# Layer 1 of a fused retention kernel takes its first two token blocks in turns, one weight chunk at a time

## The chip, the cores and the metric

The kernel runs on one core of a Trainium2 chip. The time is that of one launch on the device, in microseconds (us). TensorE does the matrix products; VectorE (DVE in the profile), ScalarE (ACT) and GpSimd (POOL) do the elementwise work; SyncE (SP) issues the transfers between DRAM and the core's memory.

## What is computed

A retention block and two layers, on 4 x 576 = 2304 tokens:

```python
scores = scale * np.matmul(q, k.transpose(0, 1, 3, 2))        # 4 batches, 8 heads, 576 x 576, head size 64
ret = scores * Dmat                                            # gamma_h ** (i - j) for i >= j, else 0
x = np.matmul(ret, v)                                          # -> 2304 tokens x 512
h = x @ w_in1;  x = (h * np.tanh(softplus(h))) @ w_out1        # layer 1: 512 -> 2048 -> 512, Mish
h = x @ w_in2;  out = (h / (1 + np.exp(-1.702 * h))) @ w_out2  # layer 2: 512 -> 2048 -> 512
```

The weights arrive as 64-bit floats and are turned into 32-bit ones on the core. For precision each operand of a layer's product is kept as a high part that TensorE takes and a low part, the rest; a product is made of three (high x high, high x low, low x high: PARTS).

## The kernel before

**Retention** (attention(), L678) walks 20 units: 4 batches of five chunks of tokens, four of 128 and one of 64. A unit's q, k, v are one transfer of 1 MB (0.5 MB for the short one) into one of four buffers (load, L682; load(u + 3) is issued in iteration u). TensorE makes scores (L738), the state's update (L761) and the outputs (L786, L797); VectorE masks the scores (L742) and writes x (finish, L811); POOL scales v (decay_v, L727). In iterations 17 and 18 the first two up-products of layer 1 follow.

**Layer 1** goes over SLOTS: one slot is one block of tokens (BLOCKS, 512 or 256 wide) with one chunk m of the 2048 hidden values (16 chunks of 128). In step i TensorE does up(i), 12 products into a PSUM bank, and down(i - 3), 12 products onto four accumulators (LAG = 3); elementwise(i) puts Mish on ScalarE, splits the result g into high (ScalarE) and low (VectorE, or POOL for i < POOL_SLOTS = 9). The order before, with m in brackets: block 0 [0-7], block 1 [0-15], block 0 [8-15], block 2 (256 wide) [0-15], block 3 [0-7], block 4 [0-15], block 3 [8-15]. A slot that begins another block needs its x split into high and low first (split_x, L336), into buffers that the last up of the block before must have left; the accumulators of a block that ends are moved to X by VectorE (evacuate, L378).

**Chunks.** A chunk's weights (1 MB of 64-bit words) are fetched in two halves into the buffer of the next chunk (fetch, L166) and turned by convert (L224), each half in stages that are spread over the following steps: clamp (L189, VectorE), rest and rebase (ScalarE for chunks 0 to 5; rebase on VectorE, L194, from chunk 6 on), sign (L134, L201, VectorE), join (L205, POOL), the high part (ScalarE), the low part by subtraction (L247, VectorE for chunks 0 to 5, POOL from 6 on). EARLY = 6 chunks are fetched during retention, one every three units from unit 2 on; the others start at the slots LATE. plan() gives each job its step and position() runs it there: "fetch", "pool", "act early", "vector", "act late" are fixed places in every step. The program order of each engine is written out by hand in this way (manual_schedule), and each engine works its own in order.

**Layer 2's weights** are prepared during slots PREP_FIRST = 23 to PREP_LAST = 67 (prepare, L255: 32 jobs, four buffers "cr") and written to DRAM as a stream that layer 2 (second_layer, L530) reads back.

## Time and profile before

| | us |
|---|---|
| runs | 852.04, 853.03, 854.59; median 853.03 |
| the profiled execution | 857.23, its span 855.4 |
| TensorE busy (PE) | 830.4 (97%) |
| VectorE busy (DVE) | 585.8 (68%) |
| ScalarE busy (ACT) | 389.5 (46%) |
| GpSimd busy (POOL) | 153.7 (18%) |

The profile is one execution; its span goes from the first to the last event on the core. PE is a product on TensorE, PEld the load of its weights; busy shares are means over the three stages. L352 is line 352 of the kernel, and one line can be a helper's: L125 is every ScalarE operation. A wait in brackets names what ended it.

### The profile page before, as it was taken

What the parts mean: (1) busy time and instruction counts of PE and PEld (TensorE: products, weight loads), DVE (VectorE), ACT (ScalarE), POOL (GpSimd) and SP (SyncE); (2) the same over time, 40 slices, a digit from 0 to 9 for tenths busy, and PEclk for the clock granted to TensorE, in tenths of its full rate; (3) what the DMA queues carried; (4) which work ended last, traced back from release to release, by engine and by line L of the source; (5) the groups of instructions that cost most, each with busy time, mean ns of one, the idle gap of its engine ahead of it and who ended that gap; (6) DMA issues with size and microseconds to landing.
All of it is one profiled execution on the core that took longest, in us unless ns stands there. A gap on an engine that the chain in (4) does not pass through costs nothing.

```text
span 855.4 us, 13241 instructions
## 1 busy us (share of the span) xinstructions
PE 830.4 (97%) x4966; PEld 749.3 (88%) x4966; DVE 585.8 (68%) x1047; ACT 389.5 (46%) x722; POOL 153.7 (18%) x154
## 2 busy tenths in 40 slices
PE   8898999999999989999999999999999999999998
PEld 5776878887887988888888899999999999999997
DVE  3697797973477876778863445588755699555776
ACT  3453544443353645455543333366333565233553
POOL 2353484642121112323310000000000000000000
PEclk9999999999999999999999999999999999999999
DMA  7899530001146775659832247778878678877774
GB/s 294 323 357 371 220 127 1 1 1 49 50 149 200 249 240 156 202 181 283 250 117 93 99 148 258 258 229 273 273 267 272 235 248 281 302 243 257 239 258 167
DMA packets 97839, 175.80 MB, mean 206 GB/s; under 512 B 5616, under 2 KB 68720, under 8 KB 92272
## 3 DMA queue, kind: packets, MB, share of 16 engines
q1 hardware_dynamic: 97776, 174.97, 60.7%
q8 instruction: 39, 0.64, 0.3%
q14 instruction: 24, 0.20, 0.1%
HBM read 140.87 MB, written 34.08 MB: 205 GB/s over the span
## 4 chain that ended last, share of the span: by engine, by line
PE 82%; DMA 6%; DVE 5%; ACT 3%; issue 2%; POOL 1%; SPq 0%; ACTq 0%; POOLq 0%; DVEq 0%
PE acc L370 20%; PE p L583 19%; PE h L352 19%; PE p L639 19%; DMA unit<-qkv_dram 5%; PE sc L738 1%; PE o L786 1%; PE o L797 1%; ACT g L125 1%; ACT cr L125 1%; PE ds L761 1%; POOL cy L205 1%; DVE cr L134 1%; DMA cr<-w_dram 1%; DVE g L429 1%
## 5 line engine op out<-in xcount | busy, mean ns | idle before, releaser
L352 PE MATMUL h<-x,w 128*128 128x512 f32 (+1 forms) x960 | 215.3, 373 | 6.4 <-ACT x L125 2.4
L370 PE MATMUL acc<-g,w 128*128 128x512 f32 (+1 forms) x960 | 212.4, 371 | 0.3 <-DVE X L388 0.3
L352 PEld LDWEIGHTS h<-x,w 128*128 128x128 f32 x960 | 169.6, 191 | 40.1 <-DVE x L340 3.1
L370 PEld LDWEIGHTS acc<-g,w 128*128 128x128 f32 x960 | 170.1, 190 | 31.6 <-issue 0.5
L639 PE MATMUL p<-g,ring 128*128 128x384 f32 x1008 | 178.8, 336 | 1.9 <-ACT g L125 0.9
L639 PEld LDWEIGHTS p<-g,ring 128*128 128x128 f32 x1008 | 174.3, 188 | 6.0 <-DVE g L429 2.4
L583 PE MATMUL p<-xop,ring 128*128 128x384 f32 x1008 | 175.2, 334 | 0.0
L583 PEld LDWEIGHTS p<-xop,ring 128*128 128x128 f32 x1008 | 174.8, 188 | 0.1
L125 ACT ACTIVATE g<-cs 128x384 fp32r<-128x384 f32 x168 | 86.9, 523 | 62.5 <-PE p L639 60.8
L429 DVE TENSOR_TENSOR g<-cs,g 128x384 fp32r<-128x384 f32 x168 | 91.8, 556 | 31.8 <-ACT g L125 31.0
L398 DVE TENSOR_TENSOR g<-c,g 128x512 fp32r<-128x512 f32 (+1 forms) x71 | 48.5, 683 | 83.3 <-ACT g L125 83.3
L125 ACT ACTIVATE g<-c 128x512 fp32r<-128x512 f32 (+1 forms) x80 | 47.2, 589 | 127.5 <-PE acc L370 127.1
L125 ACT ACTIVATE cs<-cs 128x384 f32<-128x384 f32 x72 | 37.8, 526 | 118.7 <-DVE cs L429 118.7
L205 POOL TENSOR_TENSOR cy<-cr 128x256 int32<-128x256 int32 x64 | 51.2, 820 | 159.6 <-DVE cr L201 75.7
L125 ACT ACTIVATE c<-h 128x512 f32<-128x512 f32 (+1 forms) x80 | 44.0, 550 | 56.0 <-PE h L352 55.2
L429 DVE TENSOR_TENSOR cs<-cs 128x384 f32<-128x384 f32 x96 | 53.1, 553 | 0.8
L125 ACT ACTIVATE cr<-cr 128x512 int32<-128x512 uint32 (+1 forms) x68 | 40.8, 650 | 0.5 <-DVE cr L189 0.5
L292 DVE TENSOR_TENSOR cy<-cy,cr 128x896 fp32r<-128x896 f32 x32 | 37.9, 1191 | 4.4 <-ACT cr L125 3.5
L429 DVE TENSOR_TENSOR u<-p,s 128x384 f32<-128x384 f32 x30 | 16.7, 556 | 35.3 <-PE p L583 35.3
L205 POOL TENSOR_TENSOR raw<-raw 128x512 int32<-128x512 int32 x30 | 34.5, 1150 | 34.8 <-DVE raw L201 34.8
L285 DVE TENSOR_TENSOR cy<-cy 128x128 f32<-128x128 f32 x96 | 25.4, 292 | 16.8 <-POOL cy L205 15.7
L125 ACT ACTIVATE cr<-cy 128x896 fp32r<-128x896 f32 x32 | 29.9, 942 | 12.9 <-DVE cy L286 12.9
(62 smaller groups left out, 680.1 us busy)
## 6 DMA issues: line engine op xcount, KB each, us to landing
ring<-stream SPq DMA_DIRECT2D x112, 512.0 KB, 4.5
ring<-stream SPq DMA_DIRECT2D x28, 1024.0 KB, 4.8
cr<-w_dram SPq DMA_DIRECT2D x32, 512.0 KB, 4.2
unit<-qkv_dram SPq DMA_DIRECT2D x15, 1024.0 KB, 6.8
raw<-w_dram SPq DMA_DIRECT2D x30, 512.0 KB, 8.9
stream<-cr SPq DMA_DIRECT2D x32, 448.0 KB, 2.9
stream<-cy SPq DMA_DIRECT2D x32, 448.0 KB, 3.3
unit<-qkv_dram SPq DMA_DIRECT2D x6, 512.0 KB, 5.9
```

The source lines that it names most:

```text
L125: nc.scalar.activation(out=o, in_=i, func=f, scale=scale, bias=bias)
L134: nc.vector.scalar_tensor_tensor(out=o, in0=i0, scalar=s, in1=i1, op0=op0, op1=op1)
L205: nc.gpsimd.tensor_tensor(out=o, in0=upper, in1=bits, op=ALU.add)
L285: nc.vector.tensor_tensor(out=v[:, o], in0=v[:, a], in1=v[:, b], op=op)
L292: nc.vector.tensor_tensor(out=y, in0=v, in1=hi.bitcast(F32), op=ALU.subtract)
L352: nc.tensor.matmul(h[:, :n], lhsT=W[m][:, a, k * P : (k + 1) * P], rhs=xs[k][:, b, :n], start=((k, a, b) == order[0]), stop=((k, a, b) == ...
L370: nc.tensor.matmul(acc[e][:, :n], lhsT=W[m][:, a, DM + e * P : DM + (e + 1) * P], rhs=g[:, b, :n], start=(begins(i) and a == 0 and b == 0) ...
L398: lambda: eng.tensor_tensor(out=g[:, 1, :n], in0=c[:, :n], in1=g[:, 0, :n].bitcast(F32), op=ALU.subtract),
L429: eng.tensor_tensor(out=o, in0=a, in1=b, op=op)
L583: nc.tensor.matmul(banks[p], lhsT=w[:, a, k * P : (k + 1) * P], rhs=x[:, b, k], start=(p not in SAME and k == 0 and a == 0 and b == 0), st ...
L639: nc.tensor.matmul(banks[e, p], lhsT=w[:, a, e * P : (e + 1) * P], rhs=g[:, b], start=(p != 2 and r == 0 and a == 0 and b == 0), stop=(r = ...
L738: nc.tensor.matmul(sc[j][:n, p, :n], lhsT=kt[sl, p, :], rhs=qt[sl, p, :], start=True, stop=True)
```

## The change

- SLOTS: the blocks are now 512, 256, 512, 512, 512 wide. Blocks 0 and 1 (SIDE, 256 wide) take turns: chunk 0 for block 0, chunk 0 for block 1, chunk 1 for block 0, and so on. Then block 2 takes all chunks, block 3 half of them, block 4 all, block 3 the other half. A slot has a third field, the stretch it belongs to, by which begins() and ends() go.
- SIDE's x stands in two buffers of its own ("side0", "side1"), split in retention at units 13 to 16 (X_UNITS); its accumulators share two banks (b4, b5), so that "up" has two banks, b6 and b7, until four slots after the pair.
- The x of block 2 is split in elementwise(30), one slot before the pair ends.
- EARLY: 4 chunks in retention instead of 6, one every four units, converted five units later; the other 12 are planned 1.95 slots apart from slot 1. Chunk 15 comes in halves instead of quarters.
- The unit buffers: five instead of four, load(u + 4) in iteration u.
- rebase is always on ScalarE, the weight subtractions and the g subtractions always on VectorE.
- Layer 2's weights are prepared over slots 28 to 68. The "cr" buffers are two; the other two jobs of four use side0 and side1 once the pair is done. Later the same two hold a tile each of layer 2 (g2, t3); "u4" has two buffers.

```diff
--- before.py
+++ after.py
@@ -26,35 +26,26 @@
 CH = [(c, min(P, S - c)) for c in range(0, S, P)]
 NCH = len(CH)
 UNITS = [(b, c) for b in range(B) for c in range(NCH)]
-BLOCKS = [(0, 512), (512, 512), (1024, 256), (1280, 512), (1792, 512)]
-PAIRS = [(0, 1), (3, 4)]
-OTHER = {t: u for p in PAIRS for t, u in (p, p[::-1])}
+BLOCKS = [(0, 512), (512, 256), (768, 512), (1280, 512), (1792, 512)]
+SIDE, WIDTH = 1, 256
+OTHER = {3: 4, 4: 3}
 HALF = NM // 2
-def slots():
-    order = []
-    for t in range(len(BLOCKS)):
-        if any(t == p[0] for p in PAIRS):
-            order += [(t, range(HALF)), (t + 1, range(NM)), (t, range(HALF, NM))]
-        elif t not in OTHER:
-            order.append((t, range(NM)))
-    return [(t, m) for t, ms in order for m in ms]
-SLOTS = slots()
+SLOTS = [(t, m, t) for m in range(NM) for t in (0, SIDE)] + [(2, m, 2) for m in range(NM)]
+SLOTS += [(3, m, 3) for m in range(HALF)] + [(4, m, 4) for m in range(NM)] + [(3, m, 5) for m in range(HALF, NM)]
+BOTH = 2 * NM
 def begins(i):
-    return i < len(SLOTS) and (i == 0 or SLOTS[i][0] != SLOTS[i - 1][0])
+    return i < len(SLOTS) and all(SLOTS[j][2] != SLOTS[i][2] for j in range(i))
 def ends(i):
-    return 0 <= i < len(SLOTS) and (i + 1 == len(SLOTS) or begins(i + 1))
+    return 0 <= i < len(SLOTS) and all(s[2] != SLOTS[i][2] for s in SLOTS[i + 1 :])
 def sources(o, n):
@@ -68,9 +59,11 @@
 LAG = 3
 KEPT = 10
-EARLY = 6
-EARLY_FIRST, EARLY_EVERY = 2, 3
-LATE = (1, 3, 5, 6.5, 8, 10, 12, 14, 15.5, 17)
+X_UNITS = (6, 8, 10, 12, 13, 14, 15, 16)
+EARLY = 4
+EARLY_EVERY, EARLY_AFTER = 4, 5
+LATE = [1 + 1.95 * i for i in range(NM - EARLY)]
+UNITS_AHEAD = 4
@@ -89,9 +82,8 @@
 UP_STEPS = NR * NP
 STEPS = 2 * UP_STEPS
 AHEAD = 3
-PREP_FIRST, PREP_LAST = 23, 67
+PREP_FIRST, PREP_LAST = 28, 68
 X_FIRST = 75
-POOL_SLOTS = 9
 WARM = 3
@@ -208,23 +200,18 @@
         lower, bits = words(raw)[:2]
         act(bits, lower, scale=2.0**-29)
-    def parts(m, i, q):
+    def parts(m, i):
         if m not in W:
             W[m] = place(m).tile([P, 2, 2 * DM], F32R, tag=f"w{m}", name=f"w{m}")
-        n = q * DM // 2
-        w = W[m][:, :, i * n : (i + 1) * n].rearrange("p r (q n) -> p r q n", q=q)
+        w = W[m][:, :, i * DM : (i + 1) * DM].rearrange("p r (q n) -> p r q n", q=2)
         return w[:, 0], w[:, 1]
-    def quarter(m, j):
-        raw = temp[0].tile([P, 1, DM // 2], I64, tag="cr", name="cr", bufs=4)
-        nc.sync.dma_start(out=raw[:, 0], in_=w1[m][:, j * DM // 2 : (j + 1) * DM // 2])
-        return raw
-    def convert(m, i, q, engine):
-        if q == 1:
-            raw = quarter(m, i)
+    def convert(m, i):
+        if m == NM - 1:
+            raw = temp[0].tile([P, 2, DM // 2], I64, tag="cr", name="cr", bufs=2)
+            nc.sync.dma_start(out=raw, in_=w1[m][:, i * DM : (i + 1) * DM].rearrange("p (q n) -> p q n", q=2))
             yield "skip"
             yield "vector"
         else:
@@ -233,7 +220,7 @@
         clamp(raw)
         yield "act early"
         rest(raw)
-        rebase(raw, nc.vector if m >= EARLY else nc.scalar)
+        rebase(raw, nc.scalar)
         yield "vector"
         sign(raw)
         yield "pool"
@@ -241,10 +228,10 @@
         yield "act late"
         if i == 0:
             W.pop(m, None)
-        hi, lo = parts(m, i, q)
+        hi, lo = parts(m, i)
         act(hi, value)
-        yield "pool" if engine is nc.gpsimd else "vector"
-        engine.tensor_tensor(out=lo, in0=value, in1=hi.bitcast(F32), op=ALU.subtract)
+        yield "vector"
+        nc.vector.tensor_tensor(out=lo, in0=value, in1=hi.bitcast(F32), op=ALU.subtract)
     def pause(columns):
@@ -252,12 +239,15 @@
             yield "skip"
             columns -= BLOCKS[SLOTS[slot[0]][0]][1]
-    def prepare(r, part, half):
-        while live["cr"] == 4:
+    def prepare(j, r, part, half):
+        while live["cr"] == 4 or (j % 4 > 1 and slot[0] < BOTH):
             yield "act late"
         live["cr"] += 1
-        raw = temp[0].tile([P, 4, P], I64, tag="cr", name="cr", bufs=4)
+        if j % 4 > 1:
+            raw = keep.tile([P, 4, P], I64, tag=f"side{j % 2}", name="cr")
+        else:
+            raw = temp[0].tile([P, 4, P], I64, tag="cr", name="cr", bufs=2)
         nc.sync.dma_start(out=raw, in_=w2[r, part, half])
         yield from pause(NB)
         yield "vector"
@@ -302,49 +292,53 @@
     last = [-n_u]
-    def plan_conversion(m, s, every, engine):
-        if m == NM - 1:
-            for i in range(4):
-                plan("fetch", max(s - 1, last[0]) + i * 4 / 3, convert(m, i, 1, engine))
-            return
+    def plan_conversion(m, s, every):
         for i in range(2):
             last[0] = max(math.ceil(s + i * every / 2), last[0] + (i == 0))
-            plan("vector", last[0], convert(m, i, 2, engine))
+            plan("fetch" if m == NM - 1 else "vector", last[0] - (m == NM - 1), convert(m, i))
     for m in range(EARLY):
-        u = int(EARLY_FIRST + EARLY_EVERY * m)
+        u = EARLY_EVERY * m
         plan("fetch", u - n_u, fetch(m))
-        plan_conversion(m, u + 1 - n_u, 2, nc.vector)
+        plan_conversion(m, u + EARLY_AFTER - n_u, 2)
     for m, s in zip(range(EARLY, NM), LATE):
         if m < NM - 1:
             plan("fetch", s - 2.5 if m + 1 < KEPT else max(s - 2.5, 0), fetch(m))
-        plan_conversion(m, s, 2, nc.gpsimd)
+        plan_conversion(m, s, 2)
     times = [0]
     for i in range(PREP_FIRST, PREP_LAST):
         times.append(times[-1] + BLOCKS[SLOTS[i][0]][1])
     for i in range(4 * NR):
         s = max(j for j, t in enumerate(times) if t <= times[-1] * i / (4 * NR - 1))
-        plan("act late", PREP_FIRST + s, prepare(i // 4, i // 2 % 2, i % 2))
-    xs, hs, gs, acc = {}, {}, {}, {}
+        plan("act late", PREP_FIRST + s, prepare(i, i // 4, i // 2 % 2, i % 2))
+    xs, hs, gs, acc, side = {}, {}, {}, {}, []
     column = keep.tile([P, 32], F32, name="column")
-    def split_x(o, n, k):
-        x = xs[k] = keep.tile([P, 2, NB], F32R, tag=f"x{k}", name=f"x{k}")
+    def split_x(t, k):
+        o, n = BLOCKS[t]
+        if t == SIDE:
+            if k % 2 == 0:
+                side.append(keep.tile([P, 2, 2, WIDTH], F32R, tag=f"side{k // 2}", name="side"))
+            x = side[-1][:, k % 2]
+        else:
+            x = keep.tile([P, 2, NB], F32R, tag=f"x{k}", name=f"x{k}")
+        xs[t, k] = x
         copy(nc.vector if k % 2 else nc.scalar, x[:, 0, :n], X[:, k, o : o + n])
         return lambda: nc.vector.tensor_tensor(
             out=x[:, 1, :n], in0=X[:, k, o : o + n], in1=x[:, 0, :n].bitcast(F32), op=ALU.subtract
         )
     def up(i):
-        t, m = SLOTS[i]
+        t, m, _ = SLOTS[i]
         n = BLOCKS[t][1]
-        h = bank("h", (4, 5, 6, 7))
+        h = hs[i] = ps.tile([P, NB], F32, tag=f"b{4 + i if i < 2 else 6 + i % 2 if i < BOTH + 4 else 4 + i % 4}", name="h")
         order = [(k, a, b) for k in range(NK) for a, b in PARTS]
         if begins(i):
             order.sort(key=lambda p: p[2])
@@ -352,38 +346,43 @@
             nc.tensor.matmul(
                 h[:, :n],
                 lhsT=W[m][:, a, k * P : (k + 1) * P],
-                rhs=xs[k][:, b, :n],
+                rhs=xs[t, k][:, b, :n],
                 start=((k, a, b) == order[0]),
                 stop=((k, a, b) == order[-1]),
             )
-        hs[i] = h
     def down(i):
-        t, m = SLOTS[i]
+        t, m, _ = SLOTS[i]
         n = BLOCKS[t][1]
         if begins(i):
             for e in range(NK):
-                acc[e] = bank("acc", (0, 1, 2, 3))
+                if t != SIDE:
+                    acc[t, e] = ps.tile([P, NB], F32, tag=f"b{e}", name="acc")
+                elif e % 2 == 0:
+                    acc[t, e] = ps.tile([P, NB], F32, tag=f"b{4 + e // 2}", name="acc")
+                    acc[t, e + 1] = acc[t, e][:, WIDTH:]
         g = gs.pop(i)
         for e in range(NK):
             for a, b in PARTS:
                 nc.tensor.matmul(
-                    acc[e][:, :n],
+                    acc[t, e][:, :n],
                     lhsT=W[m][:, a, DM + e * P : DM + (e + 1) * P],
                     rhs=g[:, b, :n],
-                    start=(begins(i) and a == 0 and b == 0),
+                    start=(begins(i) and a == 0 and b == 0 and not (t == SIDE and e % 2)),
                     stop=(ends(i) and a == 1),
+                    skip_group_check=(t == SIDE),
                 )
     def evacuate(i):
-        t, m = SLOTS[i]
+        t, m, _ = SLOTS[i]
         n = BLOCKS[t][1]
         other = OTHER.get(t)
         place = BLOCKS[t if other is None else other][0]
         both = other is not None and other > t and m == NM - 1
         for e in range(NK):
-            r, a = X[:, e, place : place + n], acc[e][:, :n]
+            r, a = X[:, e, place : place + n], acc[t, e][:, :n]
             if both:
                 nc.vector.tensor_tensor(out=r, in0=a, in1=r, op=ALU.add)
             else:
@@ -392,10 +391,9 @@
     def split_g(i, c, n):
         g = keep.tile([P, 2, NB], F32R, tag="g", name="g", bufs=LAG)
         gs[i] = g
-        eng = nc.gpsimd if i < POOL_SLOTS else nc.vector
         return (
             lambda: act(g[:, 0, :n], c[:, :n]),
-            lambda: eng.tensor_tensor(out=g[:, 1, :n], in0=c[:, :n], in1=g[:, 0, :n].bitcast(F32), op=ALU.subtract),
+            lambda: nc.vector.tensor_tensor(out=g[:, 1, :n], in0=c[:, :n], in1=g[:, 0, :n].bitcast(F32), op=ALU.subtract),
         )
     def elementwise(i, jobs=True):
@@ -407,20 +405,21 @@
             c = keep.tile([P, NB], F32, tag="c", name="c", bufs=2)
             act(c[:, :n], hs.pop(i)[:, :n], AF.Mish)
-        if begins(i + 1):
-            lows = [split_x(*BLOCKS[SLOTS[i + 1][0]], k) for k in range(NK)]
+        coming = i + 1 + (i == BOTH - 2)
+        if i != BOTH - 1 and begins(coming):
+            lows = [split_x(SLOTS[coming][0], k) for k in range(NK)]
         for low in lows:
             low()
         if i < len(SLOTS):
             hi, lo = split_g(i, c, n)
             hi()
-        if i < PREP_FIRST or not begins(i + 1):
+        if i < BOTH or not begins(i + 1):
             at("act early", i)
         if lo:
             lo()
         if jobs and ends(i - LAG):
             evacuate(i - LAG)
-        if i < PREP_FIRST or not begins(i + 1):
+        if i < BOTH or not begins(i + 1):
             at("vector", i)
             at("act late", i)
@@ -438,7 +437,7 @@
         t, u = two(s)
         x11, x12, x21, x22 = X[:, 0:2, t], X[:, 0:2, u], X[:, 2:4, t], X[:, 2:4, u]
-        t3 = temp[0].tile([P, 2, TH], F32, tag="t3", name="t3")
+        t3 = keep.tile([P, 2, TH], F32, tag="side1", name="t3")
         def high(p, x):
             xop[p] = keep.tile([P, 2, 2, TH], F32R, tag=f"w{UP_ORDER.index(p)}", name="xop")
@@ -546,7 +545,7 @@
             if i % 4:
                 g = keep.tile([P, 2, TH], F32R, tag="g", name="g2", bufs=LAG)
             else:
-                g = temp[0].tile([P, 2, TH], F32R, tag="g4", name="g2")
+                g = keep.tile([P, 2, TH], F32R, tag="side0", name="g2")
             ops[i] = g
             act(g[:, 0], src)
             tt(nc.vector, g[:, 1], src, g[:, 0].bitcast(F32), ALU.subtract)
@@ -654,7 +653,7 @@
                         act(to_x(e, 11), banks[e, 1])
                         leave(e, 11)
                     elif p == 6:
-                        u2, u3, u4 = small("u2", 3), small("u3", 3), small("a", 4)
+                        u2, u3, u4 = small("u2", 3), small("u3", 3), small("u4", 2)
                         sums[e, 3], sums[e, 4] = u3, u4
                         def last(e=e, u3=u3):
@@ -684,7 +683,7 @@
                     return
                 b, c = UNITS[u]
                 n = CH[c][1]
-                t = ap.tile([P, 4 * DM], F32, tag="unit", name="unit", bufs=4)
+                t = ap.tile([P, 4 * DM], F32, tag="unit", name="unit", bufs=UNITS_AHEAD + 1)
                 e0 = 0
                 for e in (2 * DM, 4 * DM) if u == 0 else (2 * DM if n < P else 4 * DM,):
                     nc.sync.dma_start(out=t[:, e0:e], in_=qkv[b, c, :, e0:e])
@@ -717,7 +716,8 @@
             load(1)
             nc.sync.dma_start(out=gt[:, :, :P], in_=gtab)
             nc.sync.dma_start(out=steps, in_=gstep)
-            load(2)
+            for u in range(2, UNITS_AHEAD):
+                load(u)
             pm, sums, now = {}, [None], [None]
             def decay_v(u):
@@ -816,7 +816,7 @@
             decay_v(0)
             for u in range(n_u):
                 step = u - n_u
-                load(u + 3)
+                load(u + UNITS_AHEAD)
                 if u + 1 < n_u:
                     decay_v(u + 1)
                 position("pool", step)
@@ -841,8 +841,9 @@
                     scores(1)
                 position("vector", step)
                 position("act late", step)
-                if u >= NCH and (u - NCH) % 2 == 0 and u - NCH < 2 * NK:
-                    split_x(*BLOCKS[0], (u - NCH) // 2)()
+                if u in X_UNITS:
+                    k = X_UNITS.index(u)
+                    split_x((0, SIDE)[k // NK], k % NK)()
                 if u == n_u - 3:
                     up(0)
                 if u == n_u - 2:
```

## Rows read from the trace of the kernel before

**Rows 1.** The page's first line: the span of the profiled execution.

```profile
span 855.4 us, 13241 instructions
```

**Rows 2.** Timeline of TensorE: start us, us, engine, line, operation, tile, count [idle before].

```profile
12.83 1.16 PE L738 MATMUL sc<-unit 64*128 64x128 f32 x16 [2.15 <-DMA unit<-qkv_dram]
...
92.41 5.73 PE L352 MATMUL h<-x,w 128*128 128x512 f32 x24
...
122.46 2.30 PE L352 MATMUL h<-x,w 128*128 128x512 f32 x9
...
132.50 2.67 PE L352 MATMUL h<-x,w 128*128 128x512 f32 x11
...
312.02 1.60 PE L370 MATMUL acc<-g,w 128*128 128x256 f32 x12
...
320.35 1.59 PE L370 MATMUL acc<-g,w 128*128 128x256 f32 x12
...
496.14 4.17 PE L583 MATMUL p<-xop,ring 128*128 128x384 f32 x23
```

**Rows 3.** Chain of work that ended last: start us, us, what.

```profile
28.78 2.02 PE sc L738 x16
...
55.90 1.09 PE sc L738 x16
...
59.72 0.61 PE sc L738 x16
...
76.35 1.82 PE sc L738 x16
...
81.76 2.97 PE h L352 x12
...
100.86 2.72 PE h L352 x12
...
266.66 1.43 PE h L352 x12
...
357.53 2.73 PE h L352 x12
```

**Rows 4.** Waits, 0 to 96 us, and SyncE's to 100: us total, times, longest.

```profile
PE sc L738 <- DMA unit<-qkv_dram: 9.7, 5, 3.1
...
SPq L690 <- PE o L797: 52.7, 16, 6.7
```

**Rows 5.** Stretches: length, busy us of each engine (instructions), granted clock, DMA share, GB/s.

```profile
40.00:60.00 20.00, 18.12 (x280) 15.59 (x278) 19.11 (x32) 10.41 (x21) 8.84 (x9) 1.00 0.91 337
...
75.00:80.00 5.00, 3.65 (x36) 3.34 (x37) 2.37 (x5) 0.65 (x2) 3.03 (x3) 0.67 1.02 376
```

**Rows 6.** Transfers between 70 and 80 us.

```profile
DMA packets 939, 3.96 MB, mean 396 GB/s; under 512 B 103, under 2 KB 103, under 8 KB 810
```

**Rows 7.** Groups on VectorE, 20 to 78 us: shapes, count, busy us, mean ns.

```profile
L742 DVE TENSOR_TENSOR pm<-sc,cm 128x512 f32<-128x512 f32 x22 | 14.1, 680 | 2.2 <-PE sc L738 2.2
...
L134 DVE SCALAR_TENSOR_TENSOR raw<-raw 128x512 int32<-128x512 int32 x9 | 6.5, 724 | 0.3 <-ACT raw L125 0.3
L247 DVE TENSOR_TENSOR w<-raw,w 128x512 fp32r<-128x512 f32 x8 | 6.3, 786 | 0.0
L189 DVE TENSOR_SCALAR raw<-raw 128x512 f32<-128x512 f32 x10 | 4.2, 420 | 0.0
...
L201 DVE TENSOR_SCALAR raw<-raw 128x512 int32<-128x512 int32 x9 | 3.9, 429 | 0.3
```

**Rows 8.** The same view, 262 to 314 us: the narrow block.

```profile
L398 DVE TENSOR_TENSOR g<-c,g 128x256 fp32r<-128x256 f32 x14 | 6.7, 480 | 5.4 <-ACT g L125 5.4
```

**Rows 9.** The same view of VectorE and POOL, 95 to 210 us.

```profile
L205 POOL TENSOR_TENSOR raw<-raw 128x512 int32<-128x512 int32 x20 | 23.3, 1163 | 14.4 <-DVE raw L201 14.4
L201 DVE TENSOR_SCALAR raw<-raw 128x512 int32<-128x512 int32 x20 | 21.3, 1066 | 0.7
...
L247 DVE TENSOR_TENSOR w<-raw,w 128x512 fp32r<-128x512 f32 x2 | 3.6, 1780 | 0.0
```

## The prediction

> **What bounds the kernel now.** I read the page's head first: the span is 855.4 us [rows 1], and its busy shares name TensorE as the engine that is nearly always at work, so the question is where it isn't. The reader then looks at three stretches of TensorE's own timeline. (a) Retention, up to the third up-product at 92.41 us (the first two stand among the last retention units). (b) Layer 1, from there to the first product of layer 2 at 496.14 us [rows 2]. (c) Layer 2, the remaining 359 us; its products, their order and the streamed weights stay as they are, so I carry it over.
>
> For (b) the price of a slot comes from the chain of waits: twelve products of 512 columns take 2.72 us, twelve of 256 columns 1.43 us [rows 3]; each slot has twelve in "up" and twelve in "down". 64 wide slots at 5.44 and 16 narrow ones at 2.87 are 394.1 us; less the two wide ups that retention already holds, 388.7. The stretch lasted 403.7, so layer 1 loses 15.0 us. Its places: at the first change of block 122.46 to 132.50, where 5.44 was due (4.6 lost); at the change from the narrow block to the next, 312.02 to 320.35, where 4.15 was due (4.2 lost) [rows 2]; the change into the narrow block loses about as much again, and two short waits the rest. Between the changes TensorE doesn't wait.
>
> For (a): a full unit at speed takes 59.72 - 55.90 = 3.82 us [rows 3]. TensorE waited 9.7 us in five places for a unit's data [rows 4]; one of these, 2.15 us at 12.83 us [rows 2], is the third unit of a queue that has only just begun, and I leave it; 7.5 us are in reach. After two of these waits the clock was low: between 75 and 80 us the granted clock is 0.67 [rows 5], so part of that stretch ran at the lower of the two levels, 1.2 GHz, after TensorE had stood still for 3.1 us [rows 4]; the unit from 76.35 to 81.76 took 5.41 instead of 3.82, and the one at 28.78 was slow in the same way (its scores 2.02 instead of 1.09) [rows 3]. I count 1.6 for each, 3.2 together.
>
> **Part 1, retention: fewer chunks and a fifth unit buffer.** SyncE's queue held unit loads for 52.7 us in 16 waits until the output products had released a buffer [rows 4], while the transfers themselves ran near their limit: between 70 and 80 us they moved 396 GB/s [rows 6]. Five units hold 4.5 MB, and TensorE needs some 16.4 us for them at speed (an estimate: four full units, one of them without its state product, and a half one of 2.3 us). With a chunk of 1 MB every third unit that is 6.47 million bytes in 16.4 us, 394 GB/s: the limit. With one every fourth it is 6.03 million, 368 GB/s. The fifth buffer starts each load one unit (3.8 us) earlier, against waits of at most 3.1 us. So most of 7.5 + 3.2 us can go. A smaller term: the second up is now 256 wide and takes 1.43 instead of 2.72, so 1.3 us move from retention into layer 1. If all waits went, the third up would start at 92.4 - 7.5 - 3.2 - 1.3 = 80.4.
>
> What is late next is VectorE. It was busy 19.1 of 20 us between 40 and 60 us [rows 5]. From unit 6's scores, which could have started at 26.6 (28.78 less the wait before them), to 80.4, 54 us, it will hold 11 full and 3 short score maskings (22 x 0.68 + 6 x 0.48), 15 finishes (taken like the maskings, 12 x 0.68 + 3 x 0.48), 8 chunk halves of 0.72 + 0.79 + 0.42 + 0.43 = 2.36 less the last two subtractions [rows 7], and the splits of two x blocks (6 x 0.68 + 6 x 0.48; all 0.48 are the 256-wide subtraction [rows 8]): 15.0 + 2.9 + 9.6 + 17.3 + 4.1 + 2.9 = 51.8 us. Before it was about 4 us more: three halves more and no second split. It is thus 96% full, and some maskings will come late. I put the third up at 83.0 us, between 80.4 (nothing waits) and 91.1 (only the 1.3 us), nearer the first, since the sum fits and a masking may come later by the better part of a unit before TensorE waits for it.
>
> **Part 2, layer 1: turns by chunk.** With wide and narrow slots in turn, a step has one wide and one narrow run of products, 4.15 us, and a chunk serves 8.3 us of products where the first block gave it 5.44. The work from the third up on is 394.1 - 2.72 - 1.43 = 390.0. Six stretches of one block become four, with three changes into another x besides the start. At the first (pair to third block) the split of x is issued one slot early, so a narrow up, a narrow and a wide down (1.43 + 1.43 + 2.72 = 5.6 us) lie over it. The other two are between 512-wide blocks, and such a change at 357.53 cost TensorE nothing (2.73 for twelve products) [rows 3] although the preparation of layer 2's weights ran beside it. The costly changes of before had VectorE held up beside POOL's work or a narrow block as cover; both go. I take 1.5 us for what is left (0 to 6).
>
> Moved work: the weight subtractions go from POOL to VectorE, the exponent scaling from VectorE to ScalarE, nine g subtractions from POOL to VectorE. In the first layer stage the integer shift on VectorE took 1.07 us in the mean, and the weight subtractions that VectorE had itself 1.78, while POOL ran [rows 9]; in retention the same two took 0.43 and 0.79 [rows 7]. POOL keeps only the joins of 1.16 us [rows 9]. Per half chunk I take 2.36 on VectorE plus 0.7 for one operation held up by the join (0 to 1.2), 3.05; per chunk, with two slots' g subtractions (0.68 + 0.48), 7.3 us. The plan gives a chunk 1.95 steps, 8.1 us. So it fits, with three steps between a chunk's planned end and its use, and costs nothing; rivals 2 and 3 say what it costs if it doesn't fit. ScalarE gains two scalings a chunk and loses nothing; it has the same 8.1 us for them, and nothing hangs on it but those chunks. Two banks instead of four for "up" until the third block: up waits for the Mish two steps before, over 4 us old; nothing, at most the 6 us above. On SyncE's queue the chunk fetches of layer 1 stand behind the last unit load as before; layer 2's preparation starts five slots later by number and ends one later, its loads over two buffers until the pair is done and four after: nothing, since its last block of weights is still written some six slots before layer 2. The tiles that layer 2 now shares are free long before their use: nothing.
>
> One rule speaks against this part. The subtraction of 0.79 became 1.78 beside POOL [rows 7, 9]. The Trainium skill, SBUF — State Buffer, section "Who interferes with whom", says that a VectorE instruction with two SBUF inputs, as the moved subtractions are, contends with a GpSimd instruction that reads SBUF, and for its shared ports that the later of two is blocked for the whole of the other. The trace agrees in kind. By that rule each join could hold VectorE for all its 1.16 us, and a chunk would take 8.2 us of its 8.1, a delay that the three steps still cover.
>
> **Sum.** Before: 92.4 + 388.7 + 15.0 = 496.1. After: 83.0 + 390.0 + 1.5 = 474.5. The difference is 21.6 us: 9.4 at the third up, less 1.3 of work moved behind it, and 13.5 of waits inside layer 1. The profiled execution took 857.2 us (1.8 outside its span), 4.2 over the median 853.0. 857.2 - 21.6 = 835.6; for the median 831.4.
>
> **Rivals.** 1. Retention keeps its pace, because VectorE at 96% takes the place of the transfers, or because the chunk that is now fetched at once delays the first units: the third up at 91 instead of 83, 839.5 us. For it: 19.1 of 20 us; against it: 4 us less work there, and that TensorE waited for data rather than for VectorE. 22%. 2. VectorE becomes the bound of the turns by chunk. With the stretched means of before for shift and subtraction a half takes 0.42 + 0.72 + 1.07 + 1.78 = 4.0 and a chunk 9.1; twelve chunks end 12 us late, less up to 10 that three steps cover: 834 to 843. For it: these rows; against it: what stretched them was POOL's subtraction, which goes. 8%. 3. The slower side, the same in full: the join holds VectorE for 1.16 us more per half, and with 0.35 of waits for ScalarE a half takes 5.5 and a chunk 12.2: 12 x 4.1 - 10 = 39 us, 870 us. From 4.8 us per half on it is slower than before (12 x (10.8 - 8.1) - 10 = 22). Against it: half chunks of 2.4 us in retention, beside POOL's joins and its decay of v. 4%. 4. The split at the pair's end or the two banks cost what the changes of before did, 5 to 10 us: 835 to 840. For it: three such changes in the trace; against it: the cover of 5.6 us. 10%. At the other end, retention at 80.4 and no loss in layer 1 would give 827; that is the lower edge of the forecast.
>
> **How the numbers follow.** Forecast 56%, rivals 22, 8, 4 and 10%. The range from 825 to 844 leaves out the slower case, mixtures of two rivals above it, and a few per cent below. A measurement tells 0.3% from no change, so "same" is 850.5 to 855.6 us: mixtures only. Faster 0.93, same 0.03, slower 0.04.
>
> **What would show it.** Right: the third up near 83 us, at most some 3 us of waits for unit data, VectorE the releaser of what is left; shift and subtraction near 0.43 and 0.75 in the turns; no wait over 1 us between the third up and layer 2, which starts near 474 us and lasts 359. Wrong: the third up near 91 with VectorE full (rival 1); TensorE waiting for the weights of chunks 8 to 15, or for g, in the turns (2, 3); a gap at the start of the third block (4); or a longer layer 2, for which I have no term.

## The result, and the profile after

The changed kernel takes 839.8 us (median of four runs, 839.1 to 840.7) against 852.5 for the kernel before (four runs, 852.0 to 854.6): a ratio of 0.984 with a 95% interval from 0.982 to 0.986. It is 1.6% faster. The time is inside the predicted range of 825 to 844 us, in its upper half, and 8.4 us above the forecast: 12.8 us were won where 21.6 were foreseen. It is also, to 0.3 us, the time of rival 1, but not by rival 1's mechanism, as the rows show.

The page's head of the profiled execution (its time is 839.1 us) answers [rows 1]:

```profile
span 837.0 us, 13168 instructions
```

TensorE's timeline of the changed kernel answers [rows 2]: start us, us, line, operation, tile, count, and in brackets the wait before.

```profile
12.90 1.16 PE L738 MATMUL sc<-unit 64*128 64x128 f32 x16 [1.81 <-DMA unit<-qkv_dram]
...
80.56 1.85 PE L346 MATMUL h<-side,w 128*128 128x256 f32 x12 [1.01 <-ACT side L117]
...
83.79 3.06 PE L346 MATMUL h<-x,w 128*128 128x512 f32 x12
...
90.87 2.88 PE L346 MATMUL h<-x,w 128*128 128x512 f32 x12
93.59 1.59 PE L367 MATMUL acc<-g,w 128*128 128x256 f32 x12
95.02 1.60 PE L346 MATMUL h<-side,w 128*128 128x256 f32 x12
96.46 2.91 PE L367 MATMUL acc<-g,w 128*128 128x512 f32 x12
...
292.15 3.41 PE L346 MATMUL h<-x,w 128*128 128x512 f32 x12
295.39 2.91 PE L367 MATMUL acc<-g,w 128*128 128x512 f32 x12
...
336.22 0.61 PE L346 MATMUL h<-x,w 128*128 128x512 f32 x2
337.37 2.46 PE L346 MATMUL h<-x,w 128*128 128x512 f32 x8 [0.54 <-DVE x L123]
340.35 1.10 PE L346 MATMUL h<-x,w 128*128 128x512 f32 x2 [0.52 <-DVE x L333]
341.29 2.90 PE L367 MATMUL acc<-g,w 128*128 128x512 f32 x12
...
477.55 58.43 PE L582 MATMUL p<-xop,ring 128*128 128x384 f32 x336
```

The third up stands at 83.8 us where 83.0 was foreseen. The second up, at 80.56, waited 1.0 us for ScalarE's split of the narrow block's x, for which the forecast had no term. In the turns the starts are 2.72, 1.43, 1.44 and 2.75 us apart: no wait at all for 32 slots, and none at the end of the pair. Layer 1 lasts 477.55 - 83.79 = 393.8 us, of which 390.0 are work: 3.8 are lost, not 1.5. They lie at two changes of block: 292.15 to 295.39 (0.5 over 2.72) and 336.22 to 341.29 (2.4 over), the rest in tenths. Layer 2 lasts 359.4, as before.

The waits of the changed kernel up to 96 us (total, times, longest) answer [rows 4].

```profile
PE sc L738 <- DMA unit<-qkv_dram: 1.8, 1, 1.8
PE o L797 <- DVE pm L742: 1.5, 5, 0.7
```

Of the waits for data only the third unit's is left. In their place stand five short ones for VectorE's maskings, 1.5 us as against 0.5 in the kernel before, as foreseen. The line of the kernel before:

```profile
PE o L797 <- DVE pm L742: 0.5, 2, 0.4
```

The groups between 95 and 205 us answer [rows 9]: shapes, count, busy us, mean ns.

```profile
L197 POOL TENSOR_TENSOR raw<-raw 128x512 int32<-128x512 int32 x21 | 23.9, 1140 | 60.1 <-DVE raw L193 58.0 <-DMA raw<-w_dram 2.0
...
L234 DVE TENSOR_TENSOR w<-raw,w 128x512 fp32r<-128x512 f32 x22 | 15.1, 684 | 0.0
...
L193 DVE TENSOR_SCALAR raw<-raw 128x512 int32<-128x512 int32 x21 | 9.0, 429 | 0.7
```

The shift takes 0.43 us instead of 1.07 and the weight subtraction 0.68 instead of 1.78. POOL still does 21 joins here, but in the timeline of this stretch no shift and no weight subtraction runs at the same time as a join; of the g subtractions two do, and they take 1.21 and 0.91 us instead of 0.69 and 0.43. So retention, the turns and the durations of the moved operations look as foreseen, one change of block doesn't, and the time is 8.4 us over the forecast. By the profiled executions the gain is nearly as foreseen: 855.4 - 837.0 = 18.4 us. What doesn't fit is the execution of before that it is measured from.

### The profile page after: what moved, and what is told of

The parts are those of the page before. It is cut to its first block, busy times and chain, and to the rows that moved or that the text cites. A ratio compares the mean times of both kernels' runs of the same rounds, so it can differ in the third digit from the quotient of the medians.

```text
span 837.0 us, 13168 instructions
## 1 busy us (share of the span) xinstructions
PE 823.1 (98%) x4966; PEld 743.3 (89%) x4966; DVE 560.0 (67%) x1044; ACT 400.0 (48%) x738; POOL 113.9 (14%) x121
## 4 chain that ended last, share of the span: by engine, by line
PE 86%; DVE 7%; ACT 2%; DMA 2%; issue 1%; POOL 1%; SPq 0%; ACTq 0%; POOLq 0%
PE acc L367 22%; PE h L346 21%; PE p L582 20%; PE p L638 19%; PE o L797 1%; PE sc L738 1%; PE o L786 1%; DVE x L333 1%; DMA unit<-qkv_dram 1%; DVE pm L742 1%; ACT g L117 1%; DMA stream<-cy 1%; PE ds L761 1%; DVE g L428 1%; DVE x L123 1%
## 5 line engine op out<-in xcount | busy, mean ns | idle before, releaser
L367 PE MATMUL acc<-g,w 128*128 128x512 f32 (+1 forms) x960 | 210.0, 368 | 0.0
L346 PE MATMUL h<-x,w 128*128 128x512 f32 x768 | 186.6, 391 | 1.3 <-DVE x L123 0.5
L346 PEld LDWEIGHTS h<-x,w 128*128 128x128 f32 x768 | 143.8, 188 | 33.5 <-DVE x L333 2.8
L396 DVE TENSOR_TENSOR g<-c,g 128x512 fp32r<-128x512 f32 x80 | 54.0, 676 | 110.1 <-ACT g L117 110.1
L117 ACT ACTIVATE g<-c 128x512 fp32r<-128x512 f32 x80 | 47.2, 590 | 131.2 <-PE acc L367 131.1
L197 POOL TENSOR_TENSOR cy<-cr 128x256 int32<-128x256 int32 x64 | 54.1, 865 | 184.9 <-DVE cr L193 101.6
L117 ACT ACTIVATE c<-h 128x512 f32<-128x512 f32 x80 | 44.1, 551 | 41.3 <-PE h L346 39.5
L117 ACT ACTIVATE cr<-cr 128x512 int32<-128x512 uint32 x68 | 41.4, 663 | 1.3 <-DVE cr L181 1.3
L117 ACT ACTIVATE raw<-raw 128x512 int32<-128x512 uint32 (+1 forms) x60 | 38.0, 674 | 8.3 <-DVE raw L181 8.1
L428 DVE TENSOR_TENSOR cs<-p,u 128x384 f32<-128x384 f32 x48 | 26.7, 557 | 11.0 <-PE p L582 10.2
```

Of the source, the lines that this page charges most:

```text
L117: nc.scalar.activation(out=o, in_=i, func=f, scale=scale, bias=bias)
L197: nc.gpsimd.tensor_tensor(out=o, in0=upper, in1=bits, op=ALU.add)
L346: nc.tensor.matmul(h[:, :n], lhsT=W[m][:, a, k * P : (k + 1) * P], rhs=xs[t, k][:, b, :n], start=((k, a, b) == order[0]), stop=((k, a, b) ...
L367: nc.tensor.matmul(acc[t, e][:, :n], lhsT=W[m][:, a, DM + e * P : DM + (e + 1) * P], rhs=g[:, b, :n],  start=(begins(i) and a == 0 and b = ...
L396: lambda: nc.vector.tensor_tensor(out=g[:, 1, :n], in0=c[:, :n], in1=g[:, 0, :n].bitcast(F32), op=ALU.subtract),
L428: eng.tensor_tensor(out=o, in0=a, in1=b, op=op)
```

## Experiments

**The kernel before, once more** (b_again).

> The kernel before, unchanged, profiled once more. The execution profiled before the prediction took 857.2 us, 4.7 over the median of its kernel. Theory: the extra time lies in retention's waits for unit data, which differ from one execution to the next; an execution near 852.5 shows its third up near 88 us instead of 92.4, and layer 1's 403.7 us and layer 2's 359 us as they were. Rival: the 4.7 us lie in layer 1 or 2 (then the third up is again near 92 us and 496.1 moves), or outside the span.

It took 850.5 us, its span 848.5. TensorE's timeline (left out: all between), its waits up to 96 us, and three stretches (length, busy us of PE, PEld, DVE, ACT, POOL, granted clock, DMA share, GB/s):

```profile
87.80 5.73 PE L352 MATMUL h<-x,w 128*128 128x512 f32 x24
...
123.54 2.94 PE L370 MATMUL acc<-g,w 128*128 128x512 f32 x12
...
489.27 50.97 PE L583 MATMUL p<-xop,ring 128*128 128x384 f32 x293
```

```profile
PE sc L738 <- DMA unit<-qkv_dram: 5.4, 4, 2.2
```

```profile
20.00:40.00 20.00, 17.84 (x258) 15.69 (x256) 13.06 (x24) 9.52 (x22) 7.71 (x7) 0.91 0.88 338
40.00:60.00 20.00, 18.27 (x287) 15.72 (x284) 19.55 (x33) 10.44 (x20) 9.29 (x9) 1.00 0.93 353
60.00:80.00 20.00, 19.03 (x248) 15.97 (x244) 19.15 (x34) 10.40 (x20) 9.93 (x10) 1.00 0.97 373
```

The third up comes at 87.8 us, 4.6 earlier than in [rows 2], with 5.4 us of waits for data instead of the 9.7 of [rows 4]; and the granted clock stays at 1.00 from 60 to 80 us, where [rows 5] had 0.67 between 75 and 80. Layer 1 is 401.5 us, 2.2 shorter, against my expectation; layer 2 is the same. Most of the 2.2 us is clock as well. The products behind the first change of block, in the execution of [rows 2]:

```profile
128.38 4.28 PE L370 MATMUL acc<-g,w 128*128 128x512 f32 x12
```

The same twelve products at 123.54 above took 2.94 us. The granted clock behind this change was 0.69 there (128.4 to 133.0 us) and 1.00 here (123.5 to 126.4), after waits for x of the same length. The products behind the change into the narrow block differ in the same way, by 0.6 us. In 30 runs made beside these experiments the kernel before lies anywhere from 850.3 to 859.1 us, and the granted clock, averaged over a run, goes with the time: in one set of nine it is 0.996 in the run of 850.9 us and 0.988 in that of 859.1. The four runs of the changed kernel lie within 1.6 us, at 0.999 to 1.000. So the execution that I read had some 4 to 5 us, of waits and of time at the lower clock (1.2 GHz), that the median doesn't have, and I took them off the median.

**Four unit buffers in the changed kernel** (a_4buf).

```diff
-UNITS_AHEAD = 4
+UNITS_AHEAD = 3
```

> The changed kernel with four unit buffers instead of five. Theory: fifth buffer and fewer chunks share the gain in retention; with loads one unit later, some waits for unit data come back, third up 86 to 88 us instead of 83.9, 842 to 844 us. Rival (VectorE's lighter load alone made retention shorter): no wait for data, 840 us. Rival (the buffer alone): third up 88 or later, 844 us or more.

845.1 us (844.8 to 845.4; ratio to the kernel before 0.992, 0.989 to 0.994): 5.4 us slower than with five. The waits up to 96 us:

```profile
PE sc L738 <- DMA unit<-qkv_dram: 7.5, 6, 2.3
```

The third up is at 89.7, and the chunks are still fetched every fourth unit: fewer chunks don't help without the buffer. That is what the second rival said (the buffer alone).

**Five unit buffers in the kernel before** (b_5buf).

```diff
-                t = ap.tile([P, 4 * DM], F32, tag="unit", name="unit", bufs=4)
+                t = ap.tile([P, 4 * DM], F32, tag="unit", name="unit", bufs=5)
...
             load(2)
+            load(3)
...
-                load(u + 3)
+                load(u + 4)
```

> The kernel before with a fifth unit buffer and nothing else. Theory: a chunk every third unit still asks for 394 GB/s, so the buffer alone gives 1 to 3 us: 849.5 to 851.5 us. Rival (the buffer alone): waits for data vanish, 5 us or more, at most 847.5 us. Rival (VectorE's load alone): 852.5 us.

847.5 us (846.5 to 848.4; ratio 0.9935, 0.991 to 0.996): 5.2 us faster than its companion runs of the kernel before, more than I expected and what the first rival said. Its waits and two of its stretches:

```profile
PE sc L739 <- DMA unit<-qkv_dram: 1.5, 1, 1.5
```

```profile
20.00:40.00 20.00, 19.93 (x319) 17.36 (x316) 16.78 (x30) 11.94 (x27) 8.87 (x8) 1.00 1.01 382
40.00:60.00 20.00, 18.42 (x264) 15.50 (x263) 19.83 (x32) 9.99 (x19) 10.82 (x10) 1.00 0.98 374
```

With six chunks, one every third unit, no unit is waited for after the third. From 20 to 60 us the transfers run at 374 to 382 GB/s with a DMA share of 0.98 and more, and that is enough; in the kernel before the DMA engines stood idle part of the time (338 and 353 GB/s at shares of 0.88 and 0.93 in the same stretches of b_again). From 60 to 80 us it is the other way round, 344 GB/s here and 373 in b_again: the same bytes come earlier. Nor was 394 GB/s the limit, as I had it: between 70 and 80 us b_again moved 417.

**Six chunks in the changed kernel's retention** (a_6early).

```diff
-EARLY = 4
-EARLY_EVERY, EARLY_AFTER = 4, 5
-LATE = [1 + 1.95 * i for i in range(NM - EARLY)]
+EARLY = 6
+EARLY_EVERY, EARLY_AFTER = 3, 1
+LATE = [1 + 1.95 * i for i in range(2, 2 + NM - EARLY)]
...
-        u = EARLY_EVERY * m
+        u = 2 + EARLY_EVERY * m
```

> The changed kernel with six chunks in retention, one every third unit from unit 2 on, as before; the later ones keep their slots. Theory: transfers and VectorE are both over what TensorE's pace leaves; third up 87 to 89 us, 843 to 845 us. Rival (the fifth buffer alone): third up near 84 us, 840 us.

840.5 us (840.2 to 842.6; ratio 0.987, 0.984 to 0.989): 0.7 us over the changed kernel, whose runs overlap with these, so the rival is right and my theory is wrong on this point. The waits up to 96 us show where two more chunks are felt:

```profile
PE o L797 <- DVE pm L742: 3.8, 7, 2.0
...
PE sc L738 <- DMA unit<-qkv_dram: 1.4, 1, 1.4
```

VectorE's maskings come later (3.8 us instead of 1.5), the third up is at 85.7 instead of 83.8; data isn't waited for.

**The weight subtractions back on POOL** (a_pool): only chunks 4 to 15, in the changed kernel.

```diff
-        rebase(raw, nc.scalar)
+        rebase(raw, nc.vector if m >= EARLY else nc.scalar)
...
-        yield "vector"
-        nc.vector.tensor_tensor(out=lo, in0=value, ...
+        yield "pool" if m >= EARLY else "vector"
+        (nc.gpsimd if m >= EARLY else nc.vector).tensor_tensor(out=lo, in0=value, ...
```

> The changed kernel with the weight subtractions of chunks 4 to 15 back on POOL and their exponent scaling back on VectorE. Theory: shift, scaling and the g subtractions on VectorE stretch again (0.43 to about 1.0), but a step of 4.15 us still holds them, so the turns themselves lose little: 0 to 4 us, 840 to 844 us. Rival (the move off POOL is what made layer 1 shorter): waits at TensorE for g or weights in the turns, 850 us or more.

840.4 us (839.8 to 840.9; ratio 0.982, 0.980 to 0.985): 0.6 over the changed kernel, again with overlapping runs; layer 1 takes 394.7 us instead of 393.8. The groups on VectorE, and below on POOL, from 95 to 205 us:

```profile
L193 DVE TENSOR_SCALAR raw<-raw 128x512 int32<-128x512 int32 x21 | 28.0, 1332 | 0.7
L186 DVE TENSOR_SCALAR raw<-raw 128x512 f32<-128x512 f32 x21 | 24.1, 1147 | 0.7
```

```profile
L234 POOL TENSOR_TENSOR w<-raw,w 128x512 fp32r<-128x512 f32 x22 | 37.3, 1696 | 16.6 <-ACT w L117 15.8 <-DMA raw<-w_dram 0.8
```

The shift is at 1.33 us and the scaling at 1.15: VectorE is held beside POOL, and a subtraction costs 1.70 us there and 0.68 on VectorE. In the timeline the 19 shifts that run at the same time as a POOL subtraction take 1.42 to 1.44 us each, and the two that don't take 0.43. The Trainium skill, SBUF — State Buffer, section "Who interferes with whom", says that VectorE in its two-port modes contends with GpSimd for a shared pair and that the second one is blocked while the first runs; the 0.43 that became 1.33 next to operations of 1.15 and 1.70 agrees with it, though no row shows in which mode the shift ran. Yet TensorE hardly feels it: with 8.3 us a chunk VectorE has the room.

**The same move in the kernel before** (b_dve).

```diff
-        rebase(raw, nc.vector if m >= EARLY else nc.scalar)
+        rebase(raw, nc.scalar)
...
-        plan_conversion(m, s, 2, nc.gpsimd)
+        plan_conversion(m, s, 2, nc.gpsimd if m == NM - 1 else nc.vector)
...
-POOL_SLOTS = 9
+POOL_SLOTS = 0
```

> The kernel before with the weight subtractions (but the last chunk's) and the first g subtractions on VectorE and the scaling on ScalarE. Theory: VectorE's operations go back to their short times and the first change of block (122.46 to 132.50, 4.6 us lost) loses at most 2; the two changes around the narrow block lose as before: 849 to 851 us. Rival (the stretched operations don't matter for that change, it is the split's own length): 852.5 us.

850.7 us (848.7 to 853.9; ratio 0.996, 0.993 to 0.999), beside companion runs with a median of 854.2 that spread over 8 us. The timeline of TensorE where the first block ends:

```profile
111.15 0.61 PE L352 MATMUL h<-x,w 128*128 128x512 f32 x2
113.42 2.56 PE L352 MATMUL h<-x,w 128*128 128x512 f32 x10 [1.65 <-DVE w L247]
...
118.54 2.88 PE L352 MATMUL h<-x,w 128*128 128x512 f32 x12
121.26 2.88 PE L370 MATMUL acc<-g,w 128*128 128x512 f32 x12
```

The change of block (the up at 118.54) now loses nothing, where it lost 3.0 us in b_again. But one slot ahead of it TensorE waits 1.65 us for a chunk's low part, since the subtraction now stands in VectorE's queue. So it isn't shown that the stretched operations caused the whole of that loss: the new wait also gives the split of x more time. Layer 1 is 401.2 us, next to 401.5 in b_again and 403.7 in [rows 2]: what one wait gave, the other mostly took.

**Without the turns** (a_seq): the changed kernel, block 0 with all its chunks first, then the narrow block; each chunk's conversion one slot after the one before it.

```diff
-SLOTS = [(t, m, t) for m in range(NM) for t in (0, SIDE)] + ...
+SLOTS = [(t, m, t) for t in (0, SIDE) for m in range(NM)] + ...
...
-LATE = [1 + 1.95 * i for i in range(NM - EARLY)]
+LATE = [i or -1 for i in range(NM - EARLY)]
...
-        plan_conversion(m, s, 2)
+        plan_conversion(m, s, 0)
...
-        if i != BOTH - 1 and begins(coming):
+        if i != BOTH - 1 and begins(coming) and SLOTS[coming][0] != SIDE:
```

> The changed kernel without the turns: block 0 takes its 16 chunks, then the narrow block its 16, and the conversions follow at one chunk per slot, since each is due at twice the pace. Theory: a chunk needs 4.7 us on VectorE and a slot's g 0.68, 5.4 of 5.44 us, and each step has no slack, so TensorE waits for weights or g through the first 16 slots: 8 to 20 us more, 848 to 860 us. Rival (the conversions have slack enough, the turns only change the order): 840 to 842 us.

870.1 us (869.9 to 871.0; ratio 1.017, 1.014 to 1.021): 30.3 us over the changed kernel, more than I expected. The waits from 80 to 260 us and one slot of TensorE's timeline:

```profile
PE h L346 <- DVE w L234: 24.3, 13, 4.0
```

```profile
115.44 0.61 PE L346 MATMUL h<-x,w 128*128 128x512 f32 x2
117.71 2.56 PE L346 MATMUL h<-x,w 128*128 128x512 f32 x10 [1.65 <-DVE w L234]
...
122.83 0.61 PE L346 MATMUL h<-x,w 128*128 128x512 f32 x2
```

A slot lasts 122.83 - 115.44 = 7.4 us instead of 5.4: each up begins and then waits for the low part of its own chunk. Four early chunks are enough only because in the turns a chunk is due every 8.3 us instead of every 5.4. (The price holds for this plan, in which a chunk's low part is emitted one step before its use; a plan with more lead wasn't run.)

**No preparation jobs in the slot before the last** (a_clear), in the changed kernel.

```diff
-        if i < BOTH or not begins(i + 1):
+        if i < BOTH or not (begins(i + 1) or begins(i + 2)):
             at("vector", i)
             at("act late", i)
...
-PREP_FIRST, PREP_LAST = 28, 68
+PREP_FIRST, PREP_LAST = 28, 66
```

> The changed kernel with no preparation jobs on VectorE and ScalarE in the slot before the last one of a block either (they are left out only in the last one now), and the preparation planned two slots shorter to make up for it. In the changed kernel the change at 336.2 us lost 2.4 us and the one at 292.2 lost 0.7, where the split of x stood behind such jobs in VectorE's queue. Theory: these go, 2 to 3 us less, 837 us. Rival (the split's own 3 us behind the last up is what TensorE waits for): 840 us.

835.9 us (835.6 to 836.2; ratio 0.977, 0.975 to 0.980), 3.8 us under the changed kernel. First VectorE in the changed kernel, in the timeline of the change that lost 2.4 us; then TensorE's first product of layer 2 in this run:

```profile
334.77 0.82 DVE L275 TENSOR_TENSOR cy<-cy 128x128 f32<-128x128 f32 x3 [0.50 <-POOL cy L197]
...
335.83 0.69 DVE L126 SCALAR_TENSOR_TENSOR cr<-cr 128x512 int32<-128x512 int32 x1
...
336.90 0.76 DVE L123 CAST x<-X 128x512 fp32r<-128x512 f32 x2
...
337.57 3.33 DVE L333 TENSOR_TENSOR x<-X,x 128x512 fp32r<-128x512 f32 x4
```

```profile
474.37 58.43 PE L582 MATMUL p<-xop,ring 128*128 128x384 f32 x336
```

There the cast of x stood behind the jobs of the slot before, which had waited for POOL's joins, and came 0.7 us after TensorE's up at 336.22. With the jobs gone layer 1 lasts 474.37 - 83.76 = 390.6 us, 0.6 over its work and 3.2 shorter than in the changed kernel, which is most of the 3.8 us.

**The same edit in the kernel before** (b_clear).

```diff
-        if i < PREP_FIRST or not begins(i + 1):
+        if i < PREP_FIRST or not (begins(i + 1) or begins(i + 2)):
...
-PREP_FIRST, PREP_LAST = 23, 67
+PREP_FIRST, PREP_LAST = 23, 65
```

> The kernel before with the edit of the run that cleared VectorE's and ScalarE's queues ahead of a change of block (no preparation jobs in the slot before the last one of a block; preparation planned two slots shorter). Theory: what the change from the narrow block to the next lost (4.2 us, and the same in the second profile of this kernel) is the queue of preparation jobs that the split of x stands behind, not the short cover of a narrow block: it falls to at most 1.5 us, and the change into the narrow block loses less too; 847 to 850 us against 852 to 854 for the kernel before. Rival (the cover of 1.4 us is too short for a split of 3 us whatever stands ahead of it): at least 3 us stay at that change, 851.5 us or more.

859.8 us (859.1 to 865.4; ratio 1.008, 1.005 to 1.010): slower than the kernel before, which neither theory had. TensorE's timeline in and behind the narrow block:

```profile
255.88 1.85 PE L352 MATMUL h<-x,w 128*128 128x256 f32 x12
...
272.29 2.32 PE L370 MATMUL acc<-g,w 128*128 128x256 f32 x12 [2.03 <-ACT cr L125]
...
295.77 2.72 PE L370 MATMUL acc<-g,w 128*128 128x256 f32 x11 [2.34 <-DVE g L398]
...
317.09 5.49 PE L352 MATMUL h<-x,w 128*128 128x512 f32 x12 [3.85 <-ACT x L125]
322.38 1.93 PE L370 MATMUL acc<-g,w 128*128 128x256 f32 x12
```

At the change into the narrow block (255.88) the theory came true: 0.3 us is lost there, where [rows 2]'s execution had waited 1.5 us for x (at 260.80) and lost 2.9. But the same preparation in fewer slots falls on the narrow block, whose slots last only 2.9 us: TensorE now waits inside it for ScalarE (2.0 us) and for g (2.3 us), and the change behind it waits longer for x on ScalarE (3.85 us, against 2.4 in [rows 2]'s execution). The products behind that wait take 5.3 us instead of 2.7, at a granted clock of 0.50, the lower level. So the jobs in the slot before were not the whole of that loss, and whether a short cover was the rest isn't settled. That the moved preparation crowds the narrow block is the reading that fits these waits; no run tests it by itself.

**Cleared queues, and x split one unit earlier in retention** (a_best).

```diff
-X_UNITS = (6, 8, 10, 12, 13, 14, 15, 16)
+X_UNITS = (5, 7, 9, 11, 12, 13, 14, 15)
```

> The changed kernel with cleared queues ahead of the changes and, new, all splits of x in retention one unit earlier (units 5, 7, 9, 11, 12 to 15 instead of 6 to 16). In the changed kernel the second up waited 1.0 us for the narrow block's x on ScalarE at 80.6 us. Theory: that wait goes and the third up comes about 1 us earlier, 834.5 to 835.5 us. Rival (VectorE, full there, gives it back as waits for maskings): 836 us or more.

832.5 us (832.1 to 833.2; ratio 0.9745, 0.972 to 0.9765), 3.4 us under a_clear: more than I expected, and by another way. TensorE's timeline (second and third up), then its waits up to 96 us:

```profile
77.88 1.85 PE L346 MATMUL h<-side,w 128*128 128x256 f32 x12 [1.01 <-ACT side L117]
...
81.11 3.02 PE L346 MATMUL h<-x,w 128*128 128x512 f32 x12
```

```profile
PE o L797 <- DVE pm L742: 0.5, 3, 0.2
```

The wait that I aimed at, 1.0 us for the narrow x on ScalarE, is still there. What went are waits for maskings (1.7 us in a_clear, 0.5 here) and 0.8 us of the third unit's wait for its data (1.9 there, 1.1 here), a wait that this edit doesn't touch. I take it, without a run that shows it, that the splits had stood beside chunk conversions in VectorE's fullest stretch; the last 0.7 of the 2.7 us by which the third up comes earlier (83.8 in a_clear) I can't name. This is the fastest version, 2.5% under the kernel before.

**Retention as before, layer 1 as changed** (a_ret): a_6early with four unit buffers.

```diff
-UNITS_AHEAD = 4
+UNITS_AHEAD = 3
```

> The changed kernel with retention as it was before: four unit buffers and six chunks, one every third unit. What is left of the change is layer 1 (turns, work off POOL) and the narrow second up. Theory: the gain of the buffer (5 us) and the gain in layer 1 (7 to 8 us) add up, so this run has the second alone: third up 87 to 91 us, 845 to 847 us; its runs spread over some us, as those of the kernel before do. Rival (the two overlap: a late retention gives the conversions a head start): 842 us or less.

845.0 us (842.3 to 845.5; ratio 0.988, 0.985 to 0.991). The third up is at 89.8 and layer 1 lasts 394.5. This is the layer 1 part alone (with the narrow second up), 7.5 us under the kernel before of the result. With the 5.2 us that the buffer gave in b_5buf these are 12.7, and the change gave 12.8, so the two parts add up. The split is no sharper than the spread of the kernel before: beside its own companion runs, median 854.5, a_ret is 9.5 us faster. The changed kernel has now been run with each pair of the two: with five buffers 839.8 us (four chunks) and 840.5 (six), with four buffers 845.1 and 845.0. The buffer counts; the number of chunks makes no difference that these runs resolve.

## Why the prediction was right, and where it was off

**What bounds the kernel** held: TensorE, with its losses in retention and at changes of block. The work terms came out to the tenth: 2.72 and 1.43 us a run, 390.0 us for layer 1, layer 2 unchanged.

**Part 1.** The third up at 83.0 was 83.8. Of the 3.4 us over the 80.4 at which nothing more would wait, 1.5 are VectorE's maskings and 1.0 is ScalarE's split of the narrow x, which I had left out; I had given VectorE 2.6. The reason was half right: the fifth buffer does it alone (b_5buf 5.2 us, a_4buf 5.4), and the step with 394 and 368 GB/s fell, since 394 was no limit (417 in b_again). Fewer chunks in retention are worth nothing that the runs resolve (a_6early, 0.7 us). The term of 3.2 us for the clock stands in part: the granted clock, 0.67 between 75 and 80 us before [rows 5], is 1.00 from 20 to 80 us in the changed kernel. But of the two slow spots in [rows 3] b_again has only the first, so the second belonged to that execution.

**Part 2.** The turns ran without a wait, with VectorE at 0.43 and 0.68 us an operation, and without them four early chunks cost 30 us (a_seq). The 0.7 us per half chunk that I had added for an operation held up by the join didn't come, because the join never met a shift or a weight subtraction. The move off POOL, to which I gave a part of the waits that go, is worth no more than 0.6 us in the changed kernel (a_pool). The term for what is left in layer 1 was mis-sized: 3.8 us instead of 1.5. I had argued from the change at 357.53 [rows 3], which lost nothing, that a change between wide blocks is free. Whether it is depends on which preparation jobs stand in VectorE's queue just then: 2.4 us at 336.22, and once they are cleared 0.6 in the whole of layer 1 (a_clear). One free instance was no bound.

**The sum.** Here is the larger error, and it isn't in a term of the change. The 21.6 us were worked out from one execution, 4.2 us over its median, and then taken off the median. That execution's waits for data, 9.7 us, are 5.4 in another one of the same kernel (b_again), and the lower clock behind its waits, in retention and at two changes of block, is partly gone there. Against b_again the third up came 4.0 us earlier instead of the 9.4 that I had put down, and layer 1 lost 9.0 us less instead of 13.5. A loss that differs from run to run can only be won back as often as it occurs. What decides in which run the clock falls, no run here shows. Taken against its own execution the forecast was 835.6 us; with 0.8 for the third up and 2.3 for layer 1 it is 838.7, and the changed kernel's profiled execution took 839.1. That 839.8 still lies in the range is due to the room that the range left for the rivals, and not to the sum.

**The rivals.** Rival 1's time came out, 839.5, without its cause, by accident: of the 8 us that it was to keep, VectorE's maskings kept 1.0 (1.5 less the 0.5 of before). Rivals 2 and 3 didn't occur; a_pool has stretched operations like those of rival 2 (shift 1.33, scaling 1.15) and loses 0.6 us. Rival 4 occurred in a small way, at another change than the one it named.

## What to carry to other kernels

Before a gain worked out from one execution is taken off a median, look at how far that execution lies from the median, and leave out of the sum what can differ between runs: the waits for transfers, and the time at the lower clock behind them. A wait for data while the transfers seem near their limit may need one more buffer and not fewer bytes; running each of the two alone tells them apart. Where helper jobs share an in-order queue with the one step that the next block waits for, clear the queue a slot ahead of it, if the block it is moved to has room.

## What the runs showed of the hardware

From 20 to 60 us the transfers moved 374 to 382 GB/s with five unit buffers and 338 to 353 with four (b_5buf, b_again), beside the same products; the highest rate over 10 us was 417, with four.

Behind some of TensorE's waits the granted clock was low and the products slow: behind the 3.85 us of b_clear twelve products of 512 columns took 5.3 us instead of 2.7, at 0.50. Behind the first change of block, with waits of the same length, it was 0.69 in one execution of the kernel before and 1.00 in another.

With four buffers and a chunk every third unit the kernel before lay between 850.3 and 859.1 us in 30 runs, and a_ret, b_dve and b_clear spread by 3.3 to 6.3 us. With five buffers, or with four chunks, every version stayed within 2.4 us, in four to seven runs each; the best comparison is b_5buf, 1.9 us in seven runs, with the ten runs of the kernel before beside it, 6.2 us. I had not expected a buffer to settle the spread as well.
